# Smaller routing batches and later row reads in a fused attention, mixture-of-experts and SwiGLU kernel

## The chip, the core and the metric

The kernel runs on one core of one Trainium2 chip. The metric is the device time of one execution in microseconds (us), as the median of several runs; lower is better.

## What is computed

```python
attn_out = _attn_ref(q, k, v)             # 4 x 8 heads, 576 positions, 64 wide, window 128, ALiBi
x = attn_out ... reshape(2304, 512)
logits = x @ w_gate
noisy = logits + log1p(exp(x @ w_noise)) * noise      # 8 experts
top2 = the two largest of noisy; top2_w = softmax over the two
for e in range(8):
    h = maximum(x[rows of e] @ w1[e], 0)              # 512 -> 1024
    out[rows of e] += top2_w * (h @ w2[e])            # 1024 -> 512
xn = out / rms(out) * rms_g
return (silu(xn @ w_gate2) * (xn @ w_val)) @ w_out    # 512 -> 1536 -> 512
```

## The kernel before

The 2304 tokens are 18 tiles of 128 (`NT`). The whole program is recorded in one order by hand (`tc.manual_schedule()`); each engine takes its instructions in that order, and a tracker puts in the waits between engines. Times depend therefore on what stands ahead of an instruction on its own engine, and on what it waits for.

**The attention loop.** A `while` loop over steps `n` (L578 onwards) runs four steps to a tile, two heads a step, as a software pipeline: scores on TensorE (L333), bias and maximum on VectorE (L344), exponentials on ScalarE (L353), transposes on TensorE (L361), products with v (L375). GpSimd makes the low halves of k, q and x (L278, L398). The last scores belong to step 69, and from step 72 (`NS`) on the loop only drains.

**Routing.** When a tile's x is done it is split in two halves, `x16`, kept in one of eight buffers, and transposed. Three steps of `logits` matmuls (L473) follow at steps 12, 16, ... 72 for tiles 0 to 15, and at steps 73 and 75 for tiles 16 and 17. When the last tile of a batch (`BATCHES`) has its logits, the generator `route` is put on a list and advances one stretch a step: softplus on ScalarE (L483), maxima on VectorE (L492, L493), chosen experts, counts on TensorE (L510, L512), and last the row numbers `slots` (L531). For each finished batch two entries per tile go to the list `todo`.

**Scatters.** `scatter(most)` takes up to `most` entries of `todo` and records for each a tiny MEMSET and one indirect DMA on GpSimd's queue (L453, L454). It writes the 128 rows of a tile into the DRAM table `xrows`, at the rows of the experts chosen. A scatter waits for `slots`, and for nothing else that is near.

**Row reads.** `row_steps` reads 128 rows of one expert from `xrows` by a transposing DMA on SyncE's queue (L178). For the first expert, rows 0 to 255 (two reads, tile `xA`) may be read once tiles 0 to 9 are scattered, rows 256 to 383 once tiles 0 to 13 are: the generator `take` sees to this and puts `rows()` on the list `taking`, which advances one stretch a step. `LANDS` is the number of steps between. A read waits for every scatter that was recorded ahead of it; scatters recorded behind an early read don't wait for it.

**The first expert's work in the loop.** `exp0` is its first layer over rows 0 to 255 and 256 to 383 (L194). Each of the 8 hidden chunks of a piece comes in two half-groups of six matmuls, so half-groups 0 to 15 are the first piece and 16 to 31 the second. From step 72 on, half-groups stand between the pieces of the draining loop; the rest of them, and the second layer (L215), run in the `drive` call behind the loop, which places side work at given counts of matmul columns. The rows from 384 on (`LAST`, tile `xB`) are read there too. The weights of the next expert come by `weights1` (DMA L111, casts L131 and L133).

Of the kernel before, what the change touches and what calls it, by code (L numbers as in the profile page):

```python
# [41 lines left out]
def attention_moe_swiglu(  # L42
# [19 lines left out]
    NT = N // P  # L62
# [81 lines left out]
    def new_weights(e):  # L144
        wts[e] = []
        return weight_steps(lambda: epool[e % 2], stage, moe_w1[e], moe_w2[e], wts[e])
# [20 lines left out]
    LAST = slice(3 * P, CAP)  # L167
# [3 lines left out]
    def row_steps(e, cs, taken=None):  # L171

        first = cs.start < GW
        if cs.start in (0, GW):
            xts[e, first] = xpiece.tile([P, 2 * KC, GW if first else CAP - GW], F16, name="xA" if first else "xB")
        for c in range(cs.start, cs.stop, P):
            at = c if first else c - GW
            ins = nc.sync.dma_start_transpose(xts[e, first][:, :, at:at + P], xrows[e * N + c:e * N + c + P, :])  # L178
            if taken is not None:
                taken.append(ins)  # L180
            yield
# [67 lines left out]
    with ExitStack() as actx:  # L249
# [106 lines left out]
        def turn(n):  # L356
            d = st[n]
            pt = d["pt"] = ps.tile([P, 2, 2, P], F32, name="mm1", bufs=MM[1])
            for j in range(2):
                for kk in range(d["k0"], 2):  # L360
                    nc.tensor.transpose(pt[:, j, kk, :], d["pr"][:, j, kk * P:(kk + 1) * P], ident)  # L361
# [6 lines left out]
        def values(n):  # L368
            d = st.pop(n)
            t, hp, k0, ph = (d[x] for x in ("t", "hp", "k0", "ph"))  # L370
            if hp % 2 == 0:
                xps[t, hp // 2] = ps.tile([P, 4, P], F32, name="acc", bufs=2)
            for j, h in enumerate(heads(hp)):
                for kk in range(k0, 2):
                    nc.tensor.matmul(xps[t, hp // 2][:, h % 4, :VN], ph[:, j, kk, :],  # L375
                                     v32[t - 1 + kk][:, h * DV:h * DV + VN], start=(kk == k0), stop=(kk == 1))
# [46 lines left out]
        def constants():  # L423
            nc.vector.tensor_scalar(wgh, wg, SG, None, op0=OP.mult)
            nc.vector.scalar_tensor_tensor(wgl, wg, SG, wgh, op0=OP.mult, op1=OP.subtract)
            yield
            nc.vector.tensor_copy(bias[1], bias[0])
            nc.gpsimd.memset(bias[1][P // 2:, :, :P + P // 2], NEG * KS)
            yield
            nc.vector.tensor_copy(bias[2], bias[0])  # L430
            nc.gpsimd.memset(bias[2][:, :, :P // 2], NEG * KS)
            yield
            nc.gpsimd.memset(ones, 1.0)
            nc.gpsimd.memset(tri, 1.0)
            nc.gpsimd.affine_select(out=tri, in_=tri, compare_op=OP.is_gt, fill=0.0, base=0,
                                    pattern=[[1, P]], channel_multiplier=-1)
            nc.gpsimd.iota(iota8, pattern=[[1, E]], base=0, channel_multiplier=0,
                           allow_small_or_imprecise_dtypes=True)
            nc.vector.tensor_scalar(gain[:, 1], gain[:, 0], SWV, None, op0=OP.mult)
            nc.vector.tensor_scalar(gain[:, 0], gain[:, 0], SWG, None, op0=OP.mult)  # L440

            for e in range(E):
                yield
                nc.sync.dma_start(xrows[e * N + CAP - P:e * N + CAP, :], x16s[0].rearrange("p a d -> p (a d)"))

        apart = acons.tile([1, 1], I32, name="apart")
        todo, scat, early_reads, mcum = [], [], [], [None]
        rt = ps.tile([P, NT + 1, 3 * E], F32, name="rt", bufs=1)

        def scatter(most):  # L450
            for t, i in todo[:most]:

                nc.gpsimd.memset(apart, 0)  # L453
                ins = nc.gpsimd.indirect_dma_start(  # L454
                    out=xrows[:, :], out_offset=bass.IndirectOffsetOnAxis(ap=slots[:, t, i:i + 1], axis=0),
                    in_=x16s[t].rearrange("p a d -> p (a d)"), in_offset=None)
                for o in scat:
                    tc.declare_no_dep(ins.ins, o.ins, reason="distinct rows")

                for o in early_reads:  # L460
                    tc.declare_no_dep(ins.ins, o.ins, reason="rows of earlier tokens")
                scat.append(ins)
                if i:
                    x16s.pop(t)
            del todo[:most]
# [73 lines left out]
        def take(i, tiles, cs):  # L539
            yield  # L540

            count = rt[:, NT, i * E:(i + 1) * E]
            nc.tensor.matmul(count, ones, mcum[0], start=True, stop=True)
            nc.vector.tensor_scalar(few[:, i:i + 1], count[:, 0:1], float(cs.stop), None, op0=OP.is_lt)
            while todo:
                scatter(2)
                yield

            def rows():
                for _ in range(LANDS[i]):  # L550
                    yield
                yield from row_steps(0, cs, early_reads)
            taking.append(rows())

        BATCHES = [(0, 3), (3, 3), (6, 4), (10, 4), (14, 2), (16, 2)]
        batch_end = {b[0] + b[1] - 1: b for b in BATCHES}
        routing, ending, taking, tasks = [], [], [], [constants()]

        def advance(steps):
            while steps:  # L560
                try:
                    next(steps[0])
                    return
                except StopIteration:
                    del steps[0]
# [5 lines left out]
        weights0, weights1 = new_weights(0), new_weights(1)  # L571
# [5 lines left out]
        n = -2  # L577
        while n < NS + HP + 2 or routing or ending or taking:  # L578
            t, p = divmod(n, HP)
            if 0 <= n + 2 < NS and n % 2 == 0:  # L580
                scores(n + 2)
            if 0 <= n < NS:
                turn(n)
            if 2 <= n < NS + 2:
                values(n - 2)
            if 0 <= n + 1 < NS:
                exps(n + 1)

            parts = [shift(n + 2)] if 0 <= n + 2 < NS else []
            if n % 2 == 0 and HP <= n < NS + 2:  # L590
                parts.append(divide((n - HP) // HP, (n - HP) // 2 % 2))
            if n == NS + 1:
                parts.append(divide(NT - 1, 1))
            for _ in itertools.zip_longest(*parts):
                pass
            if n >= NS:
                next(exp0, None)
                advance(routing)
                next(exp0, None)
                advance(ending)  # L600
                next(exp0, None)

            if 0 <= t < NT - 4 and p == 0:
                load_qkv(t + 4)
            if 1 <= t < NT - 3 and p == 0:
                load_v(t + 3)
            if 0 <= t < NT - 2 and p % 2:
                split(t + 2, p // 2, nc.gpsimd)
            for step in start.pop(n, ()):
                step()  # L610
            if p == (1 if t == NT else 3 if NT - 6 <= t - 1 < NT - 1 else 2) and 1 <= t <= NT:
                split_x(t - 1)
            if 0 <= n < NS:
                high(n)

            if p == (2 if t == NT else 3) and 1 <= t <= NT:
                put_x(t - 1)
            if n in (NS + 1, NS + 3) or p == 0 and 3 <= t < NT + 1:
                r = {NS + 1: NT - 2, NS + 3: NT - 1}.get(n, t - 3)
                logits(r)  # L620
                if r in batch_end:
                    (routing if r < NT - 1 else ending).append(route(*batch_end[r]))
                    if r + 1 in EARLY:
                        routing.append(take(list(EARLY).index(r + 1), r + 1, EARLY[r + 1]))
            advance(routing)
            advance(ending)
            advance(taking)
            if n > 2:
                advance(tasks)
            if p < 2 or n >= 60:  # L630
                scatter(1 if n < 68 else 2)
            if n > NS + 1:
                next(exp0, None)
            if n in WEIGHTS0:
                next(weights0, None)
            if n in WEIGHTS1:
                next(weights1)
            n += 1
        scatter(len(todo))


        tot = rt[:, NT, 2 * E:]
        nc.tensor.matmul(tot, ones, mcum[0], start=True, stop=True)
# [123 lines left out]
    def ahead(e):  # L767
        if e < E:
# [1 line left out]
            yield from itertools.islice(coming[e], 3)  # L770

    drive(itertools.chain(exp0, expert_steps(0, LAST)),
          (0, 2800, weights1), (16000, 0, row_steps(0, LAST)),
          (50000, 500, row_steps(1, HALVES[0])),
          (40000, 4000, mix()), (70000, 5000, ahead(2)))
    for e in range(1, E - 1):
# [409 lines left out]
```

## Time and profile before

| | |
|---|---|
| time, median of 3 runs | 973.48 us (973.41 to 974.18) |
| span of the profiled execution | 980.8 us |
| TensorE busy | 953.3 us, 97% |
| VectorE, ScalarE, GpSimd busy | 65%, 47%, 22% |

The profile is of one further execution. It gives its span, from the first to the last instruction, and no other time of its own; the span is 7.3 us more than the median of the runs. A row of the timeline has the start, the duration, the engine, the line, the operation, the tiles, the shapes, and in brackets the idle time ahead of it with what ended it. "issue" means that nothing in the trace explains the wait, "remote" that an event that is not in the trace ended it. TensorE rows merge matmuls of one line.

### The profile page before, as it was taken

How to read it: one execution, taken by the hardware profiler on the slowest of the kernel's cores; microseconds unless marked ns; L12 is line 12 of the kernel's file. 1: busy time of each engine (PE TensorE's matmuls, PEld its weight loads, DVE VectorE, ACT ScalarE, POOL GpSimd, SP SyncE). 2: the span in 40 equal slices, each digit the busy share in tenths (PEclk: the TensorE clock that was granted, in tenths of full speed). 3: DMA queues.
4: the chain of work that ended last, by engine and by line, in shares of the span. 5: the costliest groups of instructions: out<-in, count | busy, mean ns of one | idle time of the engine just before them, and what ended most of it. 6: DMA issues, size and time to landing. Idle time of an engine off the chain costs nothing.

```text
span 980.8 us, 18499 instructions
## 1 busy us (share of the span) xinstructions
PE 953.3 (97%) x7212; PEld 665.9 (68%) x7212; DVE 640.7 (65%) x1481; ACT 462.0 (47%) x935; POOL 212.0 (22%) x255
## 2 busy tenths in 40 slices
PE   7999997999999999999999998999999999999997
PEld 5998886655656565656565676588488658847864
DVE  6788764536666878778687257889258717934850
ACT  6999772534454645464543246435323522532320
POOL 5567653000000101010012224701501130130000
PEclk9999998999999999999999999999999999999999
DMA  7989763758594838495751222501521160132000
GB/s 220 311 242 243 182 178 122 196 166 239 112 273 129 243 119 246 140 239 169 216 170 44 75 66 66 127 25 34 108 66 33 28 145 1 33 64 56 1 13 35
DMA packets 145663, 126.86 MB, mean 129 GB/s; under 512 B 98208, under 2 KB 115360, under 8 KB 145568
## 3 DMA queue, kind: packets, MB, share of 16 engines
q1 hardware_dynamic: 139808, 106.73, 40.8%
q0 software_dynamic: 5760, 18.88, 5.9%
q8 instruction: 58, 0.95, 0.4%
q14 instruction: 37, 0.30, 0.1%
HBM read 76.55 MB, written 26.74 MB: 105 GB/s over the span
## 4 chain that ended last, share of the span: by engine, by line
PE 87%; issue 4%; DMA 3%; DVE 3%; ACT 1%; POOL 1%; SPq 1%; POOLq 0%; ACTq 0%; DVEq 0%
PE mm L1008 22%; PE mm L194 21%; PE acc L215 20%; PE acc L980 11%; PE acc L375 6%; PE mm L361 4%; PE mm L333 3%; DMA xq<-xg 1%; DMA ya<-ybuf,ysl 1%; SPq L909 1%; DMA raw<-in_qkv 1%; DVE sums L728 1%; PE rt L473 0%; DVE pgl L962 0%; DVE ss L344 0%
## 5 line engine op out<-in xcount | busy, mean ns | idle before, releaser
L194 PEld LDWEIGHTS <-w1h 128*128 128x128 f16 x1088 | 105.9, 100 | 39.7 <-issue 1.2
L200 DVE SCALAR_TENSOR_TENSOR hl<-mm,hh 128x256 f16<-128x256 f32 (+2 forms) x136 | 63.6, 469 | 105.5 <-ACT hh L199 104.0
L215 PE MATMUL acc<-w2h,hh 128*128 128x512 f16 x320 | 121.3, 379 | 0.0
L215 PE MATMUL acc<-w2l,hh 128*128 128x512 f16 x320 | 121.3, 379 | 0.0
L215 PE MATMUL acc<-w2h,hl 128*128 128x512 f16 x320 | 121.3, 379 | 0.0
L215 PEld LDWEIGHTS <-hh 128*128 128x128 f16 x640 | 62.6, 98 | 72.8
L194 PE MATMUL mm<-xA,w1h 128*128 128x384 f16 (+2 forms) x576 | 99.9, 315 | 0.6 <-issue 0.6
L734 POOL TENSOR_TENSOR sw<-sums,sw 128x256 f16<-128x256 f32 x28 | 25.9, 928 | 343.0 <-ACT sw L731 342.6
L199 ACT ACTIVATE hh<-mm 128x256 f16<-128x256 f32 (+2 forms) x136 | 56.3, 418 | 75.3 <-PE mm L194 66.4
L980 PE MATMUL acc<-oh__3242,pgh 128*128 128x512 f16 (+2 forms) x228 | 83.3, 368 | 0.1
L980 PE MATMUL acc<-ol__3243,pgh 128*128 128x512 f16 (+2 forms) x228 | 83.3, 368 | 0.0
L980 PE MATMUL acc<-oh__3242,pgl 128*128 128x512 f16 (+2 forms) x228 | 83.2, 368 | 0.0
L1008 PE MATMUL mm<-xq,sw 128*128 128x256 f16 x672 | 77.9, 273 | 2.9 <-DMA xq<-xg 2.9
L980 PEld LDWEIGHTS <-pgh 128*128 128x128 f16 x456 | 44.1, 98 | 49.1 <-ACT pgh L960 0.6
L375 PE MATMUL acc<-v,pf 128*128 128x96 f32 x544 | 72.8, 275 | 2.1 <-issue 2.0
L1008 PEld LDWEIGHTS <-sw 128*128 128x128 f16 x672 | 65.7, 98 | 11.1 <-issue 2.2
L375 PEld LDWEIGHTS acc<-v,pf 128*128 128x128 f32 x544 | 68.1, 195 | 2.6 <-issue 2.6
L194 PE MATMUL mm<-xB,w1h 128*128 128x256 f16 x512 | 67.7, 273 | 0.0
L344 DVE CUSTOM_DVE_ANT_0 ss<-mm,bias 128x256 f32<-128x256 f32 (+1 forms) x144 | 54.1, 397 | 19.2 <-PE mm L333 9.1
L353 ACT ACTIVATE pr<-ss,nm 128x256 f32<-128x256 f32 (+1 forms) x144 | 63.2, 489 | 6.3 <-DVE nm L344 6.2
L194 PEld LDWEIGHTS <-w1l 128*128 128x128 f16 x544 | 52.9, 100 | 18.9 <-issue 0.9
L1017 DVE TENSOR_TENSOR gt<-mm,p 128x512 f32<-128x512 f32 x24 | 16.6, 691 | 65.0 <-PE mm L1008 62.7
(201 smaller groups left out, 1867.0 us busy)
## 6 DMA issues: line engine op xcount, KB each, us to landing
st<-in_moe_w SPq DMA_DIRECT2D x64, 512.0 KB, 5.0
ybuf<-ys SPq DMA_DIRECT2D x40, 256.0 KB, 2.3
raw<-in_qkv SPq DMA_DIRECT2D x17, 512.0 KB, 5.5
st<-in_moe_w_gate SPq DMA_DIRECT2D x12, 512.0 KB
st<-in_moe_w_val SPq DMA_DIRECT2D x12, 512.0 KB
st<-in_moe_w_out SPq DMA_DIRECT2D x12, 512.0 KB
v<-in_qkv SPq DMA_DIRECT2D x18, 279.0 KB, 4.6
out<-ys SPq DMA_DIRECT2D x17, 256.0 KB, 2.2
```

The source lines that it names most:

```text
L194: nc.tensor.matmul(hp[:, :w], w1[:, c, f * P:(f + 1) * P], xT(xo + c, cs), start=(n == 0), stop=(n == 3 * KC - 1))
L199: nc.scalar.activation(hh[:, f, hs], hp[:, :w], AF.Relu)
L200: nc.vector.scalar_tensor_tensor(hl[:, f, hs], hp[:, :w], 0.0, hh[:, f, hs], op0=OP.max, op1=OP.subtract)
L215: nc.tensor.matmul(yp, hx[:, f, i * P:(i + 1) * P], w2[:, f, :], start=(n == 0), stop=(n == 3 * FC - 1))
L333: nc.tensor.matmul(st[n + i]["sp"][:, j, c:c + w * P], qT[t][ds, a, h // 2, :], kT[ds, b, h // 2, sl:sl + w, :], start=(m == 0), stop=(m = ...
L344: nc.vector.tensor_tensor_reduce(out=d["ss"][:, j, c0:], in0=d["sp"][:, j, c0:], in1=bias[kind][:, heads(d["hp"])[j], c0:], scale=-1.0 / K ...
L353: nc.scalar.activation(d["pr"][:, j, c0:], d["ss"][:, j, c0:], AF.Exp, scale=-1.0, bias=d["nm"][:, j:j + 1])
L361: nc.tensor.transpose(pt[:, j, kk, :], d["pr"][:, j, kk * P:(kk + 1) * P], ident)
L375: nc.tensor.matmul(xps[t, hp // 2][:, h % 4, :VN], ph[:, j, kk, :], v32[t - 1 + kk][:, h * DV:h * DV + VN], start=(kk == k0), stop=(kk == 1))
L734: nc.gpsimd.tensor_tensor(out=here[k][1], in0=x, in1=here[k][0], op=OP.subtract)
L980: nc.tensor.matmul(op[:, ds], px[:, f, cs], w[:, f, ds], start=(k == 0), stop=(k == 3 * GC - 1))
L1008: nc.tensor.matmul(pp, w(a, pa, c), xq[:, 4 * b + 2 * pb + c, :], start=(n == 0), stop=(n == 5))
```

## The change

Batches of routing hold two tiles each from tile 6 on. `take` scatters nothing itself any more; `rows()` waits until the tiles it needs have left `todo`. Scatters are recorded one at a time: in two steps of four up to step 63, and in every step from 64 on. What is left in `todo` at the loop's end (tiles 16 and 17, four scatters) is recorded in the `drive` behind the loop, one per 4500 columns; the read of the rows from 384 on moves there from 16,000 to 22,000 columns.

```diff
             nc.vector.tensor_scalar(few[:, i:i + 1], count[:, 0:1], float(cs.stop), None, op0=OP.is_lt)
-            while todo:
-                scatter(2)
-                yield
 
             def rows():
+                while todo and todo[0][0] < tiles:
+                    yield
                 for _ in range(LANDS[i]):
                     yield
                 yield from row_steps(0, cs, early_reads)
...
-        BATCHES = [(0, 3), (3, 3), (6, 4), (10, 4), (14, 2), (16, 2)]
+        BATCHES = [(0, 3), (3, 3), *((t, 2) for t in range(6, NT, 2))]
...
-            if p < 2 or n >= 60:
-                scatter(1 if n < 68 else 2)
+            if p < 2 or n >= 64:
+                scatter(1)
...
-        scatter(len(todo))
-
+
+        def last_rows():
+            while todo:
+                scatter(1)
+                yield
...
-          (0, 2800, weights1), (16000, 0, row_steps(0, LAST)),
+          (0, 2800, weights1), (0, 4500, last_rows()), (22000, 0, row_steps(0, LAST)),
```

Followed by hand through the generators, the steps at which things are recorded are these:

| | before | after |
|---|---|---|
| `slots` of tiles 6, 7 / 8, 9 | step 56, all four | steps 47 / 55 |
| `slots` of tiles 10, 11 / 12, 13 | step 69, all four | steps 60 / 68 |
| `slots` of tiles 14, 15 / 16, 17 | steps 74 / 77 | steps 74 / 77 |
| scatters of tiles 6 to 9 | steps 56 to 59 | steps 52, 53, 56, 57, 60, 61, 64, 65 |
| scatters of tiles 10 to 13 | steps 69 to 71 | steps 66 to 73, one each |
| scatters of tiles 14, 15 | steps 74, 75 | steps 74 to 77, one each |
| the two reads for half-group 0 (step 72) | steps 64, 65 | steps 70, 71 |
| the read for half-group 16 (step 76) | step 73 | step 75, behind the first scatter of tile 14 |

SyncE's queue around the reads of the first expert's rows (tile `xA`; `st` is a buffer for weights), before:

```order
L404 DMA_TRANSPOSE xTg<-x_2571 128x8x128
L178 DMA_TRANSPOSE xA<-xrows 128x8x128 x2
L111 DMA st<-in_moe_w 128x4x256 x3
L178 DMA_TRANSPOSE xA<-xrows 128x8x128
L111 DMA st<-in_moe_w 128x4x256
L1118 TENSOR_LOAD over
```

and with the change:

```order
L404 DMA_TRANSPOSE xTg<-x_2620 128x8x128
L178 DMA_TRANSPOSE xA<-xrows 128x8x128
L111 DMA st<-in_moe_w 128x4x256
L178 DMA_TRANSPOSE xA<-xrows 128x8x128
L111 DMA st<-in_moe_w 128x4x256 x2
L178 DMA_TRANSPOSE xA<-xrows 128x8x128
L111 DMA st<-in_moe_w 128x4x256
L1120 TENSOR_LOAD over
```

A load of weights now stands between the first two reads, and these stand behind the scatters of steps 69 and 70.

GpSimd's queue around the scatters of tiles 6 and 7 (x_1282 and x_1432), before; x_2254 is the x of tile 12:

```order
L398 TENSOR_TENSOR x_2254<-x,x_2254 128x512
L453 MEMSET apart 1x1
L454 DMA xrows<-x_1282,slots 18432x1024
L278 TENSOR_TENSOR kT<-raw,kT 128x4x128
L453 MEMSET apart 1x1
L454 DMA xrows<-x_1282,slots 18432x1024
L453 MEMSET apart 1x1
L454 DMA xrows<-x_1432,slots 18432x1024
```

and with the change, where x_2278 is the x of tile 12:

```order
L453 MEMSET apart 1x1
L454 DMA xrows<-x_1282,slots 18432x1024
L278 TENSOR_TENSOR kT<-raw,kT 128x4x128
L453 MEMSET apart 1x1
L454 DMA xrows<-x_1282,slots 18432x1024
L278 TENSOR_TENSOR qT<-raw,qT 128x512
L398 TENSOR_TENSOR x_2278<-x,x_2278 128x512
L453 MEMSET apart 1x1
L454 DMA xrows<-x_1432,slots 18432x1024
L278 TENSOR_TENSOR kT<-raw,kT 128x4x128
```

Tiles 6 to 8 go out with GpSimd's other work between them. Behind the x of tile 14, the last that GpSimd splits, its queue holds only scatters, before and after, from tile 10 and from tile 9 on; between them nothing stands but the MEMSETs, and the order of the last eight is unchanged.

## Rows read from the trace of the kernel before

**Rows 1.** Head of the page, TensorE's share and the chain that ended last.

```profile
span 980.8 us, 18499 instructions
PE 953.3 (97%) x7212; PEld 665.9 (68%) x7212; DVE 640.7 (65%) x1481; ACT 462.0 (47%) x935; POOL 212.0 (22%) x255
PE 87%; issue 4%; DMA 3%; DVE 3%; ACT 1%; POOL 1%; SPq 1%; POOLq 0%; ACTq 0%; DVEq 0%
```

**Rows 2.** Windows: length, busy of PE, PEld, DVE, ACT, POOL, granted clock, DMA, GB/s.

```profile
112.00:118.00 6.00, 6.00 (x89) 5.62 (x89) 5.38 (x22) 4.67 (x11) 5.24 (x8) 1.00 1.00 201
118.00:122.00 4.00, 2.51 (x28) 2.13 (x27) 1.86 (x10) 0.25 (x2) 3.53 (x6) 0.94 0.56 216
146.00:150.00 4.00, 2.22 (x23) 1.54 (x22) 0.00 (x0) 0.00 (x0) 3.33 (x8) 0.85 0.56 214
150.00:156.00 6.00, 5.53 (x36) 3.64 (x36) 3.40 (x16) 1.34 (x5) 0.09 (x2) 0.53 0.31 88
168.00:173.00 5.00, 4.82 (x61) 4.82 (x62) 3.31 (x17) 1.87 (x5) 2.97 (x5) 0.66 0.27 103
```

**Rows 3.** ScalarE takes up hidden chunks late, behind "remote" and at the first piece's end.

```profile
151.38 0.38 ACT L199 ACTIVATE hh<-mm 128x256 f16<-128x256 f32 x1 [5.44 <-remote]
...
165.46 0.72 ACT L199 ACTIVATE hh<-mm 128x256 f16<-128x256 f32 x3 [1.11 <-PE mm L194]
```

**Rows 4.** TensorE's logits of tiles 12 and 13, four steps apart.

```profile
118.27 0.25 PE L473 MATMUL rt<-wgh,xTg 128*128 128x16 f16 x4
...
129.16 0.25 PE L473 MATMUL rt<-wgh,xTg 128*128 128x16 f16 x4
```

**Rows 5.** GpSimd's scatters: second of tile 6, first of 10 and of 14, the last two.

```profile
114.67 1.23 POOL L454 DMA_INDIRECT xrows<-x,slots  x1 [0.17 <-issue]
...
139.93 0.99 POOL L454 DMA_INDIRECT xrows<-x,slots  x1 [10.59 <-DVE rank L533]
...
159.69 0.96 POOL L454 DMA_INDIRECT xrows<-x,slots  x1 [9.61 <-DVE rank L533]
172.13 0.96 POOL L454 DMA_INDIRECT xrows<-x,slots  x1 [0.21 <-issue]
...
173.40 0.96 POOL L454 DMA_INDIRECT xrows<-x,slots  x1 [0.21 <-issue]
```

**Rows 6.** From issue to landing: the scatters; then the reads into `xA`.

```profile
DMA to landing us min/median/max: 3.1/3.4/6.0
DMA to landing us min/median/max: 3.1/3.4/4.1
```

**Rows 7.** SyncE's issues of the reads into `xA` and `xB`.

```profile
130.67 2.64 SPq L178 DMA_TRANSPOSE xA<-xrows  x2
...
153.54 1.24 SPq L178 DMA_TRANSPOSE xA<-xrows  x1
...
178.47 4.45 SPq L178 DMA_TRANSPOSE xB<-xrows  x2
```

**Rows 8.** TensorE: half-group 0, the start of 16, the counts of the last batch, `xB`.

```profile
144.06 0.60 PE L194 MATMUL mm<-xA,w1h 128*128 128x256 f16 x4
...
163.41 0.82 PE L194 MATMUL mm<-xA,w1h 128*128 128x256 f16 x8
...
168.18 0.18 PE L510 MATMUL rt<-m,tri 128*128 128x8 f16 x1 [2.44 <-DVE m L504]
...
189.53 0.60 PE L194 MATMUL mm<-xB,w1h 128*128 128x256 f16 x4
```

**Rows 9.** One score pass and the end of one routing stretch on VectorE.

```profile
138.28 0.42 DVE L344 CUSTOM_DVE_ANT_0 ss<-mm,bias 128x256 f32<-128x256 f32 x1
...
139.69 0.17 DVE L533 TENSOR_SCALAR rank<-rank 128x8 f32<-128x8 f32 x1
```

**Rows 10.** Windows of four steps with less and with more routing work on VectorE.

```profile
95.80:103.10 7.30, 7.30 (x86) 6.59 (x85) 5.90 (x32) 7.27 (x18) 5.33 (x6) 1.00 0.90 233
103.10:110.85 7.75, 7.75 (x100) 7.05 (x99) 6.94 (x38) 7.08 (x17) 3.16 (x3) 1.00 0.67 127
```

## The prediction

> **What bounds the kernel.** Read the head of the page first [rows 1]: TensorE is busy for 97% of the span and makes 87% of the chain that ended last. Any idle stretch of TensorE, and any stretch at its lower clock, lengthens the run; the other engines count only where they make it wait. The change touches 90 to 190 us, so the windows there come next [rows 2]. Two stretches stand out. From 118 to 122 TensorE is busy 2.51 of 4 us, and the group of four steps that holds this stretch takes 129.16 - 118.27 = 10.9 us [rows 4], where a group with the same engines full takes 7.3 us [rows 10]. From 146 to 150 it is busy 2.22 of 4 us, with VectorE and ScalarE at zero, and from 150 to 156 its granted clock is 0.53, so mostly the 1.2 GHz level. Both stretches lie in a run of scatters: the scatters of tiles 6 to 9 from 114.67, those of 10 to 13 from 139.93 [rows 5]. ScalarE's wait there ended "remote" after 5.44 us [rows 3]: no producer is named.
>
> What the stretches cost: the first 10.9 - 7.3 = 3.6 us. The second 1.8 us idle (146 to 150) and 0.5 us (150 to 156), and by the clock 0.15 x 4 + 0.47 x 6 = 3.4 us, together 5.7 us. That is 9.3 us. **Do the timed runs have them?** The span is 7.3 us longer than the median of the runs, and outside of these stretches I find no place in the trace that could give so much back. Nor is it plain load on the DMA engines: from 112 to 118 they are full (share 1.00) and TensorE is busy throughout, while in the bad stretches their share is 0.56 [rows 2]. That all engines halt together, with no producer named, fits a cost of recording the trace. I take it that the timed runs mostly lack these stretches. The sum then is: span 980.8 less 9.3 gives 971.5 us, 2 us under the median of 973.5, and what the change adds is put on the median.
>
> The Trainium skill, page "Runtime: NRT & Kernel Launch", section "The ~15µs preamble/postamble breakdown", says that a profile's total stands some 6.2 us above the reported execution time whatever the kernel. No run here shows it. By that the 7.3 us would be nearly explained without the halts, and the first rival would have the better case.
>
> **The change part by part.**
>
> 1. *Scatters spread out.* Tiles 6 to 8 now go out between GpSimd's other work. The rest don't: once the x of tile 14 is made, GpSimd's queue holds nothing but scatters, and a scatter waits only for `slots`, so those of tiles 9 to 11 follow each other every 173.40 - 172.13 = 1.27 us [rows 5], faster than a step. Six in a row take 7.6 us. Without the halts this gains 0; with them the first halt moves a few steps back and the second loses its run of eight.
>
> 2. *The reads for half-group 0.* Before, they went out at 130.67 [rows 7] for matmuls at 144.06 [rows 8], with 13 us to spare. Now the second waits for the first scatter of tile 12, whose `slots` are recorded in step 68. In the trace the batch recorded in step 69 gave its first scatter at 139.93 [rows 5]. One step earlier, VectorE does it without the two score passes of that step and the two small sums ahead of them (2 x 0.35 + 2 x 0.17 [rows 9]), so about 1.05 us sooner, at 138.9. Landing takes 3.4 us, the read 3.1 us [rows 6]: 145.4, 1.3 us after TensorE wants it. All that follows on TensorE stands behind this half-group, the values of the last heads too, so nothing takes it up. With the shortest row for both it is 138.9 + 3.1 + 3.1 = 145.1, a wait of 1.0 us; with the longest 138.9 + 6.0 + 4.1 = 149.0, a wait of 4.9 us. I take 1.3, by the medians; the load of weights that now stands between the two reads shares the DMA engines with the second, and could make it more. The loads of weights come later than before, but are wanted only behind the loop.
>
> 3. *The read for half-group 16.* It waits for the first scatter of tile 14, at 159.69 [rows 5], recorded at the same step as before. 159.69 + 3.4 + 3.1 = 166.2. TensorE wants it in the middle of the row at 163.41, at about 163.85 [rows 8]: 2.3 us idle. But TensorE is idle there anyway: four half-groups later it waited 2.44 us for the counts of the last batch, to 168.18. Without the halts that chain would be ready some 1.4 us sooner, at 166.8: VectorE's work for it stands behind the last hidden chunk of the first piece, which left TensorE at about 163.85 and was taken up by ScalarE only at 165.46 [rows 3], 1.6 us later, of which I leave 0.2 for the ordinary hand-over. With the change: 166.2 plus four half-groups (1.3 us) is 167.5. Net 0.7 us; from -0.7 (the chain stays at 168.18) to 4.3 (landings of 6.0 and 4.1).
>
> 4. *The clock.* Behind the idle 2.44 us [rows 8] the granted clock fell to 0.66 from 168 to 173, which costs 0.34 x 5 = 1.7 us [rows 2]. Without the halts the kernel before would be idle there for about 1 us only, after four half-groups of work; the change makes one stretch of 2.3 us and adds the one of 1.3. Whether the clock falls behind 1.3 us no row tells. I take half of one fall, 0.9 us (0 to 3.4, two falls).
>
> 5. *Six batches for tiles 6 to 17, instead of four.* In the code a batch of two is 19 VectorE instructions and one of four is 25. Before, 2 x 25 + 2 x 19 = 88; now 6 x 19 = 114. The 26 more, at 0.17 us each [rows 9], are 4.4 us; ScalarE gets 4 more. Most of it falls into steps 41 to 60, where three batches take the place of one. There the window with 5.90 us of VectorE took 7.30, the one with 6.94 took 7.75 [rows 10]: 1 us more on VectorE cost 0.4 us. With 4.4 us that is 1.8 us; some lands in groups that have room, so 1.2 (0 to 3).
>
> 6. *The last four scatters and `xB`.* GpSimd's order of these four is unchanged, so they leave when their `slots` are there, as before: 0. The read of `xB` moves behind the first store of results, from 178.47 [rows 7]; it is wanted at 189.53 [rows 8]. The store waits for the first tile of the second layer; even 5 us later the pair (4.45 us of issue, 3.1 us landing) is in at about 189.5. Hidden, with little room: 0 (0 to 2).
>
> Sum: 1.3 + 0.7 + 0.9 + 1.2 = 4.1 us. 973.5 + 4.1 = **977.6 us**, slower by 0.42%. About 0.2%, 2 us, is what a measurement of this kernel can tell from no change.
>
> **Rivals.**
>
> *The halts are in the timed runs too.* For it: they are in the trace, and a wait without a producer need not come from recording. Against it: the 7.3 us. Then the second halt goes (-5.7), the first is only moved, since six scatters still follow each other (0), the wait for half-group 0 stays (+1.3), the one for 16 ends ahead of the late chain (-0.7), the clock falls there in both (0, and 0.5 for half-group 0), batches 1.2: -3.4, **970.1 us**, faster. It decides if more than some 5 us of the halts are real. Chance 0.2.
>
> *No change.* The landings come at the shortest, the clock doesn't fall, VectorE has room: 1.0 us is left of the first read and nothing else, **974.5 us**. For it: three of the four terms have an end at 0 or below. Against it: the batch of tile 12 has no way to be earlier than step 68. Chance 0.2.
>
> *The reads are late by a whole run.* They share the DMA engines with four scatters and a load of weights, and land at the longest rows: 4.9 for half-group 0, 2 for 16, one fall of the clock, 1.7, and the batches, 1.2, are 9.8: **983.3 us**. Chance 0.1.
>
> **How the numbers follow.** The forecast has 0.5, its own range 975.5 to 981. From 970.5 to 982.5 no more than 2 in 10 is left out. Faster by over 0.2%: nearly all of the first rival, less where only part of the halts is real, 0.17. Within 0.2%: the second rival and a little of the first, 0.23. Slower: the forecast and the third, 0.60.
>
> **What would show it.** In the profile of the changed kernel: half-group 0 waits for a DMA, the read into `xA`, by 1 to 3 us; half-group 16 likewise by about 2; the scatters of tiles 9 to 11 start 1.27 us apart; the window before step 60 has VectorE over 6.9 of 7.7 us and groups over 7.4 us; `xB` is not waited for. I am wrong if `xA` is there when TensorE asks, or if the timed runs gain with the stretch at 146 gone.

## The result and the profile after

The changed kernel takes **984.61 us** (median of 4 runs, 983.27 to 987.89) against 973.44 us (972.35 to 974.18) for the kernel before in the same comparison: ratio 1.0118, 95% interval 1.0101 to 1.0135. It is slower by 11.2 us. The forecast was 977.6 us, range 970.5 to 982.5: the sign was right, the size nearly three times too small.

The head of the page of the changed kernel, answering to [rows 1]:

```profile
span 981.6 us, 18504 instructions
PE 950.8 (97%) x7204; PEld 664.5 (68%) x7204; DVE 645.8 (66%) x1507; ACT 462.7 (47%) x939; POOL 213.2 (22%) x255
...
PE 84%; DMA 5%; DVE 4%; issue 3%; ACT 1%; POOL 1%; SPq 1%; POOLq 0%; DVEq 0%; ACTq 0%
```

TensorE has 2.5 us less busy time than in [rows 1], but the trace of [rows 1] has the halts in it. Against the kernel before without them (e0 below: span 971.3 us, TensorE busy 946.0) it is busy for 4.8 us more and idle for 5.5 us more. The share of DMA in the chain has grown from 3% to 5%. The execution profiled here took 983.34 us, 1.7 us more than its span. Windows of it, with the columns of [rows 2]:

```profile
86.00:92.00 6.00, 4.20 (x55) 3.64 (x53) 5.85 (x25) 3.70 (x9) 3.93 (x5) 1.00 0.64 133
118.00:122.00 4.00, 4.00 (x68) 3.87 (x67) 3.86 (x19) 3.95 (x10) 3.47 (x5) 1.00 0.39 150
144.00:148.00 4.00, 0.00 (x0) 0.00 (x0) 0.00 (x0) 0.00 (x0) 0.00 (x0) 0.96 1.15 281
148.00:152.00 4.00, 3.46 (x17) 2.47 (x18) 0.27 (x1) 0.38 (x1) 0.00 (x0) 0.50 0.78 239
152.00:156.00 4.00, 4.00 (x37) 3.73 (x36) 1.14 (x5) 0.78 (x3) 0.00 (x0) 0.69 0.00 0
```

Three things are to be seen. The stretch from 118 to 122, where TensorE was busy for 2.51 of 4 us in [rows 2], is full. From 144 to 148 no engine does anything while the DMA engines are full, and behind that the granted clock is at the 1.2 GHz level for a while. And from 86 to 92 TensorE is idle for 1.8 us beside a VectorE that is full (5.85 of 6 us), in a place where the prediction looked for nothing. The waits behind these, on TensorE:

```profile
90.20 0.84 PE L361 MATMUL mm<-ident,pr 128*128 128x128 f32 x4 [1.80 <-ACT pr L353]
...
148.53 1.03 PE L194 MATMUL mm<-xA,w1h 128*128 128x256 f16 x4 [5.68 <-DMA xA<-xrows]
...
169.04 0.38 PE L194 MATMUL mm<-xA,w1h 128*128 128x128 f16 x4 [2.78 <-DMA xA<-xrows]
```

The second row is half-group 0, which waits 5.68 us for its reads; the third is half-group 16, 2.78 us. What led to the second row, on GpSimd, then on SyncE, then the landing of the reads into `xA` (compare [rows 5], [rows 7], [rows 6]):

```profile
128.47 0.99 POOL L454 DMA_INDIRECT xrows<-x,slots  x1 [0.16 <-issue]
129.76 0.96 POOL L454 DMA_INDIRECT xrows<-x,slots  x1 [0.22 <-issue]
...
138.38 0.96 POOL L454 DMA_INDIRECT xrows<-x,slots  x1 [2.51 <-DVE rank L533]
```
```profile
138.49 1.23 SPq L178 DMA_TRANSPOSE xA<-xrows  x1
139.77 0.59 SPq L111 DMA_DIRECT2D st<-in_moe_w  x1
142.68 1.49 SPq L178 DMA_TRANSPOSE xA<-xrows  x1
```
```profile
DMA to landing us min/median/max: 3.1/3.9/5.6
```

The six scatters of tiles 9 to 11 follow each other every 1.27 us from 128.47, as foreseen. The first scatter of tile 12 leaves at 138.38, the second read 4.3 us behind it, and TensorE starts on its rows another 5.85 us later.

### The profile page after: what moved, and what is told of

Same layout as the page of the kernel before. It is cut to its first block, busy times and chain, and to the rows that moved or that the text cites. A ratio compares the mean times of both kernels' runs of the same rounds, so it can differ in the third digit from the quotient of the medians.

```text
span 981.6 us, 18504 instructions
## 1 busy us (share of the span) xinstructions
PE 950.8 (97%) x7204; PEld 664.5 (68%) x7204; DVE 645.8 (66%) x1507; ACT 462.7 (47%) x939; POOL 213.2 (22%) x255
## 4 chain that ended last, share of the span: by engine, by line
PE 84%; DMA 5%; DVE 4%; issue 3%; ACT 1%; POOL 1%; SPq 1%; POOLq 0%; DVEq 0%; ACTq 0%
PE mm L1010 22%; PE acc L215 20%; PE mm L194 20%; PE acc L982 11%; PE acc L375 5%; PE mm L361 3%; PE mm L333 2%; DMA xq<-xg 1%; DMA xA<-xrows 1%; SPq L911 1%; DMA yb<-ybuf,ysl 1%; DMA xrows<-x,slots 1%; DVE sums L730 1%; DMA raw<-in_qkv 1%; DVE ss L344 0%
## 5 line engine op out<-in xcount | busy, mean ns | idle before, releaser
L1031 ACT ACTIVATE p<-mm 128x256 f32<-128x256 f32 x48 | 18.3, 381 | 88.6 <-PE mm L1010 88.5
```

## The experiments

Each group of kernels ran on one chip and is compared with runs of the kernel before there. The first group (e0 to e3) and the third (f0 to f3) ran on a chip where the kernel before takes 973.5 and 973.0 us; the second (e5 to e8) on another, where it takes 984.8 us.

**e0: the kernel before, once more.** No edit.

> The kernel before, unchanged, profiled once more. Theory: the halts (the stretches at 118 and at 146 us, priced at 9.3 us) are in some executions only. Then the timed runs have spans near 971.7 us (973.4 less the 1.7 us that lie around the span in the runs of the changed kernel), and a profiled execution either has both stretches and a span near 981, or lacks them and is near 972. Rival: the halts are in every execution, every span is near 980.8, and the time of a run stands 7 us below its span.

Measured: 973.13 us, ratio 0.9999 (0.9989 to 1.0008). The profiled execution has a span of 971.3 us, and no wait like the 5.44 us "remote" of [rows 3]: in the stretches of the halts every wait of over 0.3 us on TensorE has a producer. The theory held: the timed runs lack the halts. This trace, and not the one shown ahead of the prediction, is therefore what the change is to be compared with. One wait is left in it where the first halt stood, and it has a producer:

```profile
122.07 0.61 PE L333 MATMUL mm<-kT,qT 64*128 64x256 f16 x8 [1.79 <-POOL qT L278]
```

TensorE waits 1.79 us for GpSimd's low half of q. GpSimd makes it from 120.85, behind five scatters that left from 114.55 on, 1.27 us apart but for the first pair.

**e1: the batches of two alone**, in the kernel before.

```diff
-BATCHES = [(0, 3), (3, 3), (6, 4), (10, 4), (14, 2), (16, 2)]
+BATCHES = [(0, 3), (3, 3), *((t, 2) for t in range(6, NT, 2))]
```

> The kernel before with the batches of two alone; scatters in pairs, reads at steps 62 and 63 and at 71. Theory (the late reads cost nearly all, the batches only the late score pass between steps 44 and 48): 973.4 + 2.3 = 975.7, between 974 and 977; a VectorE weight cast of about 2.7 us near 86.6 us, no wait of half-group 0. Rival (the batches' load on VectorE is the price of the change): 982 to 985. Second rival (the batches cost nothing): 973.4.

Measured: 980.15 us, ratio 1.0068 (1.0055 to 1.0081). Between the two expectations: the batches cost more than I thought, 6.6 us, and half-group 0 doesn't wait. Its profiled execution (span 976.6, 5.3 us over e0) shows the weight cast of 2.69 us again and a wait of 1.79 us behind it, and a second such place, a sum of 128 x 8 elements, 0.17 us elsewhere:

```profile
122.96 3.13 DVE L523 TENSOR_TENSOR m<-m,msum 128x8 f16<-128x8 f16 x1
```
```profile
122.67 1.16 POOL L278 TENSOR_TENSOR qT<-raw,qT 128x512 f16<-128x512 f32 x1
123.78 1.16 POOL L398 TENSOR_TENSOR x<-x,x 128x512 f16<-128x512 f32 x1
124.89 1.16 POOL L278 TENSOR_TENSOR kT<-raw,kT 128x512 f16<-128x512 f32 x1
```

VectorE's sum begins while GpSimd runs the first of three instructions back to back, and ends at 126.09, when the third has ended (126.05). Of the 5.3 us, 2.3 lie in steps 44 to 48 with the cast and 1.3 in steps 60 to 68 with the sum. Another 1.7 lie in steps 73 to 75, where the granted clock fell to 0.67 (153 to 156 us); why it fell is not shown.

**e2: the changed kernel with all three reads early.**

```diff
-LANDS = (4, 1)
+LANDS = (0, 0)
```

> The changed kernel with no steps between scatters and reads: the two reads for half-group 0 at steps 66 and 67 (behind the scatters of tile 9 and the first of tile 10), the third at step 74 ahead of the scatters of tile 14. Theory (late reads): half-group 0 no longer waits (-5.7), the clock doesn't fall behind it (-3.4), half-group 16 waits less (-0 to -2): 984.6 - 9.1 = 975.5, between 974 and 976.5. Rival (batches and spread scatters cost it): 982 to 985, with TensorE's waits elsewhere.

Measured: 975.62 us, ratio 1.0023 (1.0008 to 1.0039). As the theory had it. Half-group 0 no longer waits; nine of the eleven microseconds are gone by moving three reads by four, four and one steps.

**e3: only the reads for half-group 0 early.** `LANDS = (0, 1)`.

> As the run before in the two reads for half-group 0, but the third read stays where the change put it, behind the first scatter of tile 14. Theory: half-group 0's wait and the clock fall are gone (-9.1), half-group 16 waits some 2.8 us still, of which the late counts would have cost most: 975.5 to 977.5, 0 to 2 us above the run with all reads early. Rival: the third read is a main cost by itself, and this run stays above 979.

Measured: 975.82 us, ratio 1.0030 (1.0020 to 1.0041), 0.2 us over e2, which is no difference; but e2's runs lie up to 8.4 us apart, and some 1.7 us could hide in that. Half-group 16 waits 1.34 us for its read, and the counts that follow are then waited for by 0.26 instead of 1.76 us: the late read takes the place of the late counts. Within that noise, the two reads for half-group 0 alone carry the nine microseconds.

**e5: the last part alone**, in the kernel before.

```diff
-        scatter(len(todo))
+        def last_rows():
+            while todo:
+                scatter(1)
+                yield
...
-          (0, 2800, weights1), (16000, 0, row_steps(0, LAST)),
+          (0, 2800, weights1), (0, 4500, last_rows()), (22000, 0, row_steps(0, LAST)),
```

> The kernel before with the last part of the change alone: what is left in the list of scatters is recorded in the drive call, one per 4500 columns, and the read of xB at 22,000 columns. Theory (this part is free, as predicted): 973.4, within 0.2%. Rival (the later xB is waited for, or the scatters behind the loop delay something): 975 or more.

Measured: 985.48 us against 984.77 us, ratio 1.0008 (0.9997 to 1.0019). No difference, to 0.2%: this part is free. The absolute numbers expected don't apply: on this chip all executions of the kernel before lie between 982.0 and 986.8 us, and this kernel, its near copy, has the halts. A wait of ScalarE without a producer and a window show them where the trace ahead of the prediction had them:

```profile
122.12 0.60 ACT L366 ACTIVATE pf<-mm 128x512 f32<-128x512 f32 x1 [3.87 <-remote]
```
```profile
146.00:150.00 4.00, 1.38 (x10) 1.57 (x10) 0.00 (x0) 0.31 (x1) 3.14 (x6) 0.80 0.51 197
```

The window from 118 to 122 would not do for it: TensorE is busy there for 2.40 of 4 us in this run and for 2.28 in e0, where it waits for q instead.

**e6 and f1: the scatters of tiles 6 to 9 spread out, the batches left alone**, in the kernel before; the reads follow directly. The same kernel in the second and the third group.

```diff
-LANDS = (4, 1)
+LANDS = (0, 0)
...
-            while todo:
-                scatter(2)
-                yield
-
             def rows():
+                while todo and todo[0][0] < tiles:
+                    yield
...
-            if p < 2 or n >= 60:
+            if p < 2 or n >= 64:
                 scatter(1 if n < 68 else 2)
```

> The kernel before with its own batches, the scatters of tiles 6 to 9 one at a time between GpSimd's other work (steps 56 to 67), the reads for half-group 0 directly behind them (steps 68 and 69), the rest as before. Theory: the spread scatters take away TensorE's wait of 1.8 us for GpSimd's low half of q near 122 us, which the second profile of the kernel before shows; steps 60 to 64 take 7.4 instead of 9.3 us and no weight cast is stretched: 973.4 - 2.0 = 971.5, between 970.5 and 972.4. Rival (the spread gains nothing, as predicted): 973.4. Second rival (the reads, 4 steps later than before, are late): above 974, with a wait of half-group 0 on a DMA.

> The kernel before with spread scatters for tiles 6 to 9 and reads directly behind them, again. On a chip without the stops: 973.5 - 2.0 = 971.5, between 970.5 and 972.4; steps 60 to 64 take 7.4 us. Rival: 973.5, no gain. Where there are stops: the same as in the second group, 2.6 us above before, since the first stop only moves to the next unbroken run of scatters (tiles 8 and 9).

Measured on the chip with halts: 987.41 us, ratio 1.0025 (1.0014 to 1.0036). On the other: **970.69 us** against 973.01, ratio **0.9976 (0.9966 to 0.9985)**, faster than both kernels there. The spread gains 2.3 us: TensorE's wait for q near 122 us is gone (below, the place in f1), and steps 60 to 64 take 7.4 us. On the chip with halts the first halt only moves, from 118 to about 130 us, to the unbroken run of scatters of tiles 8 and 9.

```profile
119.46 0.83 PE L333 MATMUL mm<-kT,qT 64*128 64x256 f16 x12
...
122.98 0.83 PE L333 MATMUL mm<-kT,qT 64*128 64x256 f16 x12
```

**e7 and f2: e2 with one stretch of weight casts a step later.**

```diff
-WEIGHTS0 = (6, 7, 8, *range(9, 60, 3))
+WEIGHTS0 = (6, 7, 8, *range(9, 42, 3), 43, *range(45, 60, 3))
```

> The changed kernel with early reads (as in the run with no steps between scatters and reads), and one stretch of the first expert's weight casts moved from step 42 to step 43, where GpSimd has no elementwise work. Theory (VectorE's cast waits while GpSimd's elementwise instructions run, and the extra routing work pushed it among them): the cast of 2.69 us takes 0.7, TensorE's wait of 1.8 us near 90 us goes, steps 44 to 48 take 7.4 to 7.9 instead of 9.7 us: 975.6 - 2.0 = 973.6, between 972.5 and 974.6. Rival (VectorE is simply too full there): the group stays above 9 us and the time at 975.6.

> The changed kernel with early reads and one stretch of weight casts moved from step 42 to 43, again. On a chip without the stops: 975.6 - 2.0 = 973.6, between 972.5 and 974.6, steps 44 to 48 at 7.4 to 7.9 us. Rival (VectorE is too full there anyway): 975.6, the group above 9 us. In the second group's profile the cast was no longer stretched, but the group took 9.0 us.

Measured: 986.43 us on the chip with halts, ratio 1.0023 (1.0010 to 1.0036), and there the halts hide the question. On the other 972.98 us, ratio 0.9998 (0.9988 to 1.0009), as the theory had it in size, but not for its reason alone. VectorE and then GpSimd in f2:

```profile
87.76 1.52 DVE L496 COPY tops<-mx 128x4 f32<-128x4 f32 x1
...
89.69 0.68 DVE L133 SCALAR_TENSOR_TENSOR w2l<-st,w2h 128x512 f16<-128x512 f32 x1
```
```profile
86.95 1.17 POOL L398 TENSOR_TENSOR x<-x,x 128x512 f16<-128x512 f32 x1
88.06 1.16 POOL L278 TENSOR_TENSOR qT<-raw,qT 128x512 f16<-128x512 f32 x1
```

The cast is back at 0.68 us, but a copy of four elements a row, 0.16 us elsewhere, now takes its place and ends as GpSimd's second instruction does (89.28 and 89.22), and the next cast, at 92.41, takes 1.65 us. The group of steps 44 to 48 takes 9.0 us instead of 9.7, not 7.4 to 7.9. Between the two profiled executions 0.7 us of the gain is from here; another 1.65 us is in the steps 73 to 75 (7.20 us here, 8.84 in e2), where e2's profiled execution ran at a granted clock of 0.7 from 150 to 156 and this one didn't. Whether the other executions gained by the cast or by the clock is not shown.

**e8 and f3: the changed kernel with the loads of weights behind the reads.**

```diff
-WEIGHTS1 = range(NS - 2, NS + 1)
+WEIGHTS1 = range(NS + 1, NS + 4)
```

> The changed kernel with the three loads of weights moved from steps 70 to 72 to steps 73 to 75, so that none stands between the two reads for half-group 0. Theory A (the load shares the DMA engines with the second read, whose landing took 5.6 instead of 3.1 us): the wait of half-group 0 falls from 5.7 to some 3.5 us, the time to 984.6 - 2.2 = 982.4. Theory B (the late scatter alone sets it): wait and time stay, 984.6.

> The changed kernel with the three loads of weights at steps 73 to 75, beside the changed kernel itself. Theory A (the load shares the DMA engines with the second read): the wait of half-group 0 falls by about 2 us, and the time to 2 us under that of the changed kernel in this group. Theory B (the late scatter alone sets it): the same time within 0.2%.

**f0: the changed kernel beside it.**

> The changed kernel once more, beside its variants. On a chip where the kernel before takes 973.5 us: 984.6, half-group 0 waits 5.7 us. On a chip like that of the second group, where the kernel before takes 984.8 and whole runs of scatters stop all engines: the six scatters of tiles 9 to 11 still follow each other, so the stop stays, and the late reads cost about the same: some 990 to 995. A rival reading, that the change is there to take these stops away: 980 or less, faster than before on such a chip.

Measured: e8 991.27 us where before takes 984.77, ratio 1.0071 (1.0052 to 1.0090). In the third group f0 took 985.95 us, ratio 1.0128 (1.0111 to 1.0144), and f3 983.21, ratio 1.0103 (1.0087 to 1.0118): 2.7 us less. Theory A held. In f3 the wait of half-group 0 is shorter:

```profile
146.24 0.63 PE L194 MATMUL mm<-xA,w1h 128*128 128x256 f16 x4 [3.90 <-DMA xA<-xrows]
```

3.90 us instead of 5.68 (6.01 in f0): the load of weights between the two reads cost about 2 us of the wait. What is left is still there without it. The changed kernel itself was not run on the chip with halts, so whether it loses as much there stays open; e8, its relative, loses there too.

## Why the prediction was right or wrong

The trace of e0 (span 971.3) against that of the changed kernel (span 981.6) gives the account, 10.3 us (the medians are 11.2 apart; the profiled execution of the changed kernel took 983.34 us, 1.3 under its median). TensorE's logits, every fourth step, are the marks. The changed kernel, steps 44, 60, 64, 68, 73, 75, and then e0:

```profile
87.95 0.25 PE L473 MATMUL rt<-wgh,xTg 128*128 128x16 f16 x4
...
120.77 0.25 PE L473 MATMUL rt<-wgh,xTg 128*128 128x16 f16 x4
...
128.14 0.25 PE L473 MATMUL rt<-wgh,xTg 128*128 128x16 f16 x4
...
137.01 0.25 PE L473 MATMUL rt<-wgh,xTg 128*128 128x16 f16 x4
...
156.63 0.24 PE L473 MATMUL rt<-wgh,xTg 128*128 128x16 f16 x4
...
163.82 0.25 PE L473 MATMUL rt<-wgh,xTg 128*128 128x16 f16 x4
```
```profile
88.22 0.25 PE L473 MATMUL rt<-wgh,xTg 128*128 128x16 f16 x4
...
118.15 0.25 PE L473 MATMUL rt<-wgh,xTg 128*128 128x16 f16 x4
...
127.49 0.25 PE L473 MATMUL rt<-wgh,xTg 128*128 128x16 f16 x4
...
136.31 0.25 PE L473 MATMUL rt<-wgh,xTg 128*128 128x16 f16 x4
...
147.74 0.24 PE L473 MATMUL rt<-wgh,xTg 128*128 128x16 f16 x4
...
154.93 0.25 PE L473 MATMUL rt<-wgh,xTg 128*128 128x16 f16 x4
```

| stretch (steps) | after | e0 | difference | terms | predicted |
|---|---|---|---|---|---|
| up to 44 | 87.95 | 88.22 | -0.3 | | |
| 44 to 60 | 32.82 | 29.93 | +2.9 | 5, batches | +1.2 |
| 60 to 64 | 7.37 | 9.34 | -2.0 | 1, spread | 0 |
| 64 to 68 | 8.87 | 8.82 | 0 | | |
| 68 to 73 | 19.62 | 11.43 | +8.2 | 2 and 4, half-group 0 and clock | +2.2 |
| 73 to 75 | 7.19 | 7.19 | 0 | | |
| 75 to the end | 817.8 | 816.4 | +1.4 | 3, half-group 16; 6 | +0.7 |

**The halts: right that the timed runs lack them, and the price right by luck.** e0 has none, and its runs take the same time as all others of the kernel before there. The trace shown ahead of the prediction is 980.8 - 971.3 = 9.5 us longer, where I had 9.3, but the parts are others. The kernel before with the halts, steps 68 and 75:

```profile
137.98 0.25 PE L473 MATMUL rt<-wgh,xTg 128*128 128x16 f16 x4
...
161.58 0.25 PE L473 MATMUL rt<-wgh,xTg 128*128 128x16 f16 x4
```

Steps 60 to 64 take 10.9 us there [rows 4] and 9.3 in e0, so the first halt cost 1.6 us, not 3.6: the rest is TensorE's wait for q, which e0 has too. Steps 68 to 75 take 23.6 and 18.6 us, 5.0 for the second halt. The last 2.9 us lie behind step 75, where my price had nothing. Nor do all engines halt: GpSimd is busy for 3.53 and 3.33 of 4 us in [rows 2], mostly with scatters. And the reason that I gave, a cost of recording, isn't shown: every timed run has a span of its own, so each is recorded, and the halts come with the chip: they are in none of the eight profiled executions on the one and in all four on the other. What makes them is open. The page "Runtime: NRT & Kernel Launch" of the Trainium skill, section "The ~15µs preamble/postamble breakdown", puts a profile's total some 6.2 us above the reported time. That total is not on record here, so no run shows it. What is on record is the span, and a run's time stands 1.7 to 1.8 us above its span in every execution (983.34 and 981.6). By that, an estimate, the execution shown ahead of the prediction took some 982.5 us, 9 us more than the median, and like those on the second chip.

**Term 2, the reads for half-group 0, is the step that failed**: the mechanism was right (a DMA wait of half-group 0, the second read behind the first scatter of tile 12), the size was not: 1.3 us predicted, 5.68 measured, and 4.9 at the end of its range. The sum of the two landings is where most of it went. From the scatter to the matmul I took 3.4 + 3.1 = 6.5 us; it was 4.30 + 5.85 = 10.15 (10.47 in f0, as 3.04 + 7.43), so 3.65 more. Of these, 0.3 were lost in the working: 3.1 is the shortest row of the reads, and their median is 3.4 [rows 6]. Another 1.8 are the load of weights that shares the DMA engines, which the prediction named and priced at nothing: in f3, without it, the same way takes 8.37 us, from this row to the matmul at 146.24.

```profile
137.87 0.96 POOL L454 DMA_INDIRECT xrows<-x,slots  x1 [2.51 <-DVE rank L533]
```

What makes up the other 1.6 was not tested; three more scatters leave in that time. The remaining 0.7 of the difference is in when the scatter leaves. I had it 144.06 - 138.9 = 5.2 us ahead of TensorE's need; it was 4.5 (148.53 - 5.68 = 142.85, less 138.38). The halt of [rows 4] was in both of the times that I read, and so has no part in it: in e0 the half-group and the first scatter of tile 10 each come 1.7 us sooner than in [rows 8] and [rows 5].

```profile
142.39 0.60 PE L194 MATMUL mm<-xA,w1h 128*128 128x256 f16 x4
```
```profile
138.25 0.99 POOL L454 DMA_INDIRECT xrows<-x,slots  x1 [9.24 <-DVE rank L533]
```

In e0, where the routing is recorded a step later, the scatter leaves 4.1 us ahead of the need. The step earlier thus brought 0.3 us and not 1.05, mostly since VectorE, without the two score passes, waits for TensorE's logits of step 68 instead (changed kernel):

```profile
137.50 0.19 DVE L528 TENSOR_TENSOR oh<-oh,rt 128x32 f32<-128x32 f32 x1 [0.46 <-PE rt L473]
```

e2 and e3 show the price of this term with its clock: some 9 us. My third rival, with this very cause, came to 983.3 us, and I gave it 0.1. That it came so near is in part luck: it, too, lacked 1.7 of the 2.9 us that term 5 cost and the 2.0 that term 1 gave back.

**Term 4, the clock: right in kind, a third of the size.** From 148 to 156 the granted clock was 0.50 and 0.69. From half-group 0 to the logits of step 73 the changed kernel took 8.10 us (148.53 to 156.63), e0 5.35 (142.39 to 147.74): 2.75 us, in place of 0.9. With the 5.68 of the wait, and 0.2 less on the way from step 68 to half-group 0, these are the 8.2 of the account. Behind the wait of half-group 16 the clock did not fall (1.00 from 168 to 172).

**Term 3: the mechanism held, twice the size.** +1.4 against 0.7 in the account, within its range. The 0.2 between e3 and e2 says little of it: in both profiled executions the granted clock fell in steps 73 to 75, which gave the read some 1.7 us more time.

**Term 5, the batches: mis-sized, and for another reason than I gave.** Steps 44 to 60 cost 2.9 us, not 1.2. The 26 instructions were counted right (1507 against 1481), but 2.3 of the 2.9 us lie in one group, steps 44 to 48. VectorE, GpSimd and ScalarE there, in the changed kernel:

```profile
86.57 2.69 DVE L133 SCALAR_TENSOR_TENSOR w2l<-st,w2h 128x512 f16<-128x512 f32 x1
89.19 0.41 DVE L344 CUSTOM_DVE_ANT_0 ss<-mm,bias 128x256 f32<-128x256 f32 x1
```
```profile
86.43 1.17 POOL L398 TENSOR_TENSOR x<-x,x 128x512 f16<-128x512 f32 x1
87.54 1.16 POOL L278 TENSOR_TENSOR qT<-raw,qT 128x512 f16<-128x512 f32 x1
```
```profile
89.64 0.91 ACT L353 ACTIVATE pr<-ss,nm 128x256 f32<-128x256 f32 x2 [2.30 <-DVE nm L344]
```

The routing of tiles 6 and 7, recorded ahead of the cast, moves its start from 85.75 in e0 (where it takes 0.68 us) to 86.57, just behind the start of GpSimd's instruction. It then ends 0.6 us behind GpSimd's second (88.70), the score pass behind it is late by the 2.0 us that the cast took longer, ScalarE waits, and TensorE stands idle for the 1.80 us of the row above. A rule of the Trainium skill bears on this, page "SBUF — State Buffer", section "Who interferes with whom": a VectorE instruction with two inputs in SBUF contends with a GpSimd instruction that reads SBUF, a copy or cast in certain modes does too, and the one that comes later waits until the other has ended. The trace agrees: the sum in e1 and the copy in f2 end with GpSimd's work too, while the score passes, which read TensorE's result, take 0.41 us beside GpSimd as without it. It goes further: the cast here waited for two of GpSimd's instructions and the sum in e1 for three, so VectorE did not get in between them. The order of the starts doesn't settle every case, though: in e1 another cast starts at 128.84, 0.2 us ahead of GpSimd's next such instruction, and takes 1.67 us instead of 0.43. The price of a moved VectorE instruction thus hangs on where it falls against GpSimd more than on its count. e1 pays 6.6 us for the same batches, of which 3.6 lie, in its profiled execution, in the steps with stretched instructions.

**Term 1: wrong in the other direction.** I wrote 0 since the scatters spread out only in part. With the halts gone from the trace there is still the wait of 1.79 us for q, which I had counted with the halt, and the spread takes it away: -2.0 us in the account, -2.3 by f1. **Term 6: right**, by e5, though the sum for `xB` doesn't come out from its own figures: 178.47 + 5 + 4.45 + 3.1 is 191.0, later than the 189.53 at which it was wanted. In the changed kernel TensorE doesn't wait for `xB`.

## What to carry to other kernels

When a read is moved behind a later producer, price it with the transfers that are put between and with landings longer than the longest in view: here 13 us between the reads' issue and their use became a wait of nearly 6, where the longest rows gave 4.9. And take the times from an undisturbed execution, since a stretch that is put down to a halt can hide a wait that is the kernel's own. A small instruction on VectorE can cost two microseconds if it pushes a cast or copy behind a running GpSimd instruction; so line the two queues up against each other, and don't only count instructions. Last, take the parts of a change apart: the spread scatters of this one gain 2.3 us by themselves on the chip without halts, with the old batches and early reads.

## What the runs showed that I had not expected

The same kernel before takes 973 us on one chip and 985 us on another, where long runs of scatters stand beside halts of TensorE, VectorE and ScalarE; a gain of 0.24% on the first chip (f1) is a loss of 0.25% on the second (e6). In e7 on that chip the halt is seen in the windows: TensorE 0.25 of 2 us, then 0.52 of 4 us, with the DMA engines full. (They are not always: the share was 0.56 in [rows 2].)

```profile
134.00:136.00 2.00, 0.25 (x2) 0.19 (x1) 0.00 (x0) 0.00 (x0) 1.00 (x2) 1.00 1.12 270
136.00:140.00 4.00, 0.52 (x4) 0.34 (x4) 3.29 (x16) 1.88 (x4) 0.00 (x0) 0.62 0.96 275
```

The granted clock doesn't follow from an idle stretch alone. Behind TensorE's wait of 1.57 us near 150 us it stayed at 1.00 in e0 and fell to 0.71 in e2 (windows of e0, then of e2); behind the wait of 1.8 us near 90 us it stayed in the first profile of the changed kernel and fell to 0.72 in f0, where steps 44 to 48 then took 11.2 instead of 9.7 us. These two falls were worth about 1.6 and 1.5 us.

```profile
151.00:154.00 3.00, 3.00 (x34) 2.74 (x32) 1.43 (x7) 1.68 (x3) 0.96 (x1) 1.00 0.48 101
```
```profile
150.00:153.00 3.00, 1.95 (x14) 1.44 (x14) 1.26 (x7) 0.39 (x1) 0.00 (x0) 0.71 1.14 216
```
